# A fused convolution and two feed-forward layers on one core: weight decoding moved wholly into the convolution, its inverse stages one chunk later, the filter's second transform in three reduced-precision passes

## The chip, the cores and the metric

One core of a Trainium2 chip runs the whole program in one launch. The metric is device time in microseconds (us), start to end of one execution. The median of three runs of the kernel before is 3027.79 us (3024.66 to 3028.4).

## The reference

The reference has three parts, one after the other. `L = 2 * S`, with S = 12480 positions, 2 batches and 128 channels.

```
h_filt = (maximum(pos_emb @ w1, 0) @ w2) * exp(-0.01 * pos)[:, None]
Uf = rfft(x * v, n=L, axis=1);  Hf = rfft(h_filt, n=L, axis=0)
y  = irfft(Uf * Hf, n=L, axis=1)[:, :S, :]
x1 = (x * y).reshape(24960, 128)
h  = x1 @ moe_w_in;   g = where(h > 0, h, exp(minimum(h, 0)) - 1);  x2 = g @ moe_w_out
h  = x2 @ moe2_w_in;  g = h * cos(h);                               out = g @ moe2_w_out
```

The feed-forward width is 2048. The four weight matrices arrive as 64-bit floats, as pairs of 32-bit words; the kernel has to turn them into 32-bit floats on the chip ("decoding").

## The kernel before, in words

The program has four stretches: the filter's taps (a small network, at the start), the convolution, layer 1 of the feed-forward part and layer 2.

**Convolution** (L310 to L434). The 128 channels are worked off in 32 chunks of four (`DC`, `NCH`). For each chunk there are three signals, written `k`: 0 and 1 are the two batches, 2 is the filter. Each goes through a two-step forward transform: `st_a` multiplies by a 98-row table on TensorE (tile `ps_a`), VectorE forms two products with the twiddle table (`za`, `zb`) and GpSimd (POOL) adds them (`z_t`); `st_b` multiplies by the 128-row table `dft_t` (tile `ps_b`). For `k` = 2 ScalarE (ACT) copies the result out as `hr` and `hi_f`; for `k` = 0 and 1 VectorE multiplies it with these in three instructions (`ya`, `ps_b`, `y_t`), ScalarE rounds `y_t` to the short format `yh`, and `lo_y` on POOL forms the rest `yl`. The inverse goes back in two steps: `st_c` multiplies `yh` and `yl` by the rounded tables `dft_h`, `dft_l` in three passes (tile `ps_c`), VectorE forms `wa` and `wb`, POOL adds them to `w_t`; `st_d` multiplies by `g_t` (tile `ps_d`), and VectorE multiplies by x (`at`, L407), which SP stores to `xt_d`. `prod` on POOL makes the inputs `u_t`. `st_a` and `st_b` use full 32-bit operands, `st_c` the short format (fp32r).

The order in each chunk's turn is a table written out by hand, `steps` (L424); each entry names a stage, how many chunks back it works, and `k`. The scheduler keeps program order on each engine. `ps_a`, `ps_b` and `ps_c` have one buffer each, `ps_d` two; `za`, `zb` and `w_t` have two, `wa` and `wb` one.

**Decoding** (class `Decode`, L96). A job takes 128 x n weights. VectorE works on the upper words (`sg`, `mag`, `keep`, `bits`, `av`, `pw`; L119 to L141), ScalarE squares and converts (`sq`, `lf`), and the value is split into a rounded part `hi` and a rest `lo`, which go to `w_d` in DRAM (some also whole, to `wf_d`). Layer 1's 16 jobs of 256 columns run in the convolution, one step at a time (`next(now, None)`, L432) after nine of the entries of a turn, VectorE's six instructions and POOL's three or four each. Layer 2's eight jobs of 512 columns run inside layer 1 of the feed-forward part (`arena`, L592; `next(later, None)`, L626), with two more subtractions and additions on VectorE (L161, L163).

**Feed-forward layers** (L496 to L639). Tiles of 480 tokens (`T`), 52 per layer; each has eight blocks `m` of two 128-wide slices. `gemm1` makes `h_ps` in three passes, ScalarE and VectorE make the activation, POOL splits it into `gh` and `gl` (L93, L94), `gemm2` accumulates `o_ps` five blocks later (`LAG`). `split_x` on POOL makes `xh`, `xl` of the next tile in the middle of a tile. The first weights of layer 1 are loaded by ScalarE's queue (L611), with the first two `x_in`; the first of these waits for the stores of `xt_d`.

```
steps = ((st_a, 0, 2), (st_b, 1, 1), (lo_y, 1, 0), (st_d, 2, 1), (prod, 0, 1), (st_a, 0, 0),
         (lo_y, 1, 1), (prod, -1, 0), (st_c, 1, 0), (st_b, 0, 2), (st_a, 0, 1),
         (st_c, 1, 1), (st_b, 0, 0), (st_d, 1, 0))
```

Of the kernel before, what the change touches and what calls it, by code (L numbers as in the profile page):

```python
# [74 lines left out]
def hyena_moe_kernel(ctx: ExitStack, tc: tile.TileContext, x, v, pe, w1, w2,  # L75
# [20 lines left out]
    class Decode:  # L96


        def __init__(self, alloc, n, layer, which, q):
# [25 lines left out]
        def split(self):  # L125
            self.hi, self.lo = self.t("hi", F32R), self.t("lo", F32R)
            if not self.wide:
                self.av = self.raw
                copy_r(self.hi, self.raw)
                yield  # L130
                return
            keep, bits, self.av, pw, self.bv = (self.t("keep", I32), self.t("bits", I32), self.t("av", F32),
                                                self.t("pw", I32), self.t("bv", F32))
            nc.vector.tensor_scalar(keep, self.sq, TINY * TINY, -1.0, op0=ALU.is_ge, op1=ALU.mult)
            yield
            nc.vector.scalar_tensor_tensor(bits, self.mag, 0x40000000, self.sg,
                                           op0=ALU.bitwise_xor, op1=ALU.bitwise_or)
# [8 lines left out]

        def store(self):
            l, wh, n, p = self.layer, self.which, self.n, self.o
            nc.sync.dma_start(w_d[l, wh, 0, :, p:p + n], self.hi.bitcast(F32))
            for m in FULL[l] if wh else ():  # L150
                o = m * 256 - p
                if 0 <= o < n:
                    full = self.av[:, o:o + 256]
                    if self.wide:
                        full = self.t("full", F32)[:, 0:256]
                        nc.gpsimd.tensor_tensor(full, self.av[:, o:o + 256], self.bv[:, o:o + 256], op=ALU.add)
                        yield
                    nc.sync.dma_start(wf_d[l, m], full)
            if self.wide:
                dv = self.t("dv", F32)  # L160
                self.e.tensor_tensor(dv, self.av, self.hi.bitcast(F32), op=ALU.subtract)  # L161
                yield
                self.e.tensor_tensor(self.lo, dv, self.bv, op=ALU.add)  # L163
            else:
                nc.gpsimd.tensor_tensor(self.lo, self.av, self.hi.bitcast(F32), op=ALU.subtract)
            yield
            nc.sync.dma_start(w_d[l, wh, 1, :, p:p + n], self.lo.bitcast(F32))

        def run(self):
            for part in (self.words, self.split, self.store):  # L170
                yield from part()

    with tc.manual_schedule():
        with ExitStack() as cs:
# [132 lines left out]
            with ExitStack() as vs:  # L307
# [370 lines left out]
```

## Time and profile before

| | |
|---|---|
| median of three runs | 3027.79 us |
| profiled execution: device time | 3032.04 us |
| profiled execution: span, first to last instruction | 3030.2 us |
| mean granted TensorE clock | 0.993 of full |
| busy share of the span: TensorE, its weight loads, VectorE, ScalarE, POOL | 98%, 76%, 85%, 66%, 85% |
| convolution, first `st_a` to the last store landed | 50.68 to 745.18 us |
| layer 1, first `h_ps` | 740.19 us |

The busy shares are means over four stretches with different limits, so the profile has to be read stretch by stretch. TensorE's busy time counts matmuls whose ends are modelled; a share near 100% over a stretch means that it never ran dry there.

### The profile page before, as it was taken

The page shows a single profiled execution, that of the slowest core. Times are in us where ns is not written, and L with a number is a line of the kernel's source. Part 1 is how long each engine was busy: PE and PEld are TensorE (multiplying, and loading weights), DVE is VectorE, ACT ScalarE, POOL GpSimd, SP SyncE. Part 2 cuts the span into 40 slices and gives each one's busy share as a digit, 9 for nine tenths or more (in the row PEclk, how much of TensorE's full clock was granted, in tenths as well). Part 3 has the DMA queues.
Part 4 walks back from the last instruction along what each step waited for, and adds up shares of the span by engine and source line. Part 5 has one row for each costly group of instructions (what it writes and reads, how often), then busy time and mean ns, then how long its engine had stood idle before and what let it go on. Part 6 is the DMA issues. An engine that isn't in the chain of part 4 may idle for free.

```text
span 3030.2 us, 38341 instructions
## 1 busy us (share of the span) xinstructions
PE 2966.4 (98%) x13140; PEld 2317.9 (76%) x13140; DVE 2587.9 (85%) x3272; ACT 2006.6 (66%) x3076; POOL 2575.1 (85%) x1632
## 2 busy tenths in 40 slices
PE   8999999998999999999999999999999999999999
PEld 6777677775777777888888887787888878888887
DVE  5999987876999998888888888788888888888887
ACT  2111111112887888888888888788888888888887
POOL 4888877775898998888888888888888888888888
PEclk9999999998999999999999999999999999999999
DMA  3232322222011100000000001000000000000000
GB/s 103 76 84 78 87 63 64 63 53 88 24 38 38 45 21 10 14 10 14 10 14 11 14 11 40 23 14 10 14 11 13 11 14 10 14 11 14 11 14 14
DMA packets 79635, 96.16 MB, mean 32 GB/s; under 512 B 5722, under 2 KB 63096, under 8 KB 79442
## 3 DMA queue, kind: packets, MB, share of 16 engines
q1 hardware_dynamic: 74016, 88.07, 10.0%
q10 hardware_dynamic: 5426, 5.65, 0.6%
q8 instruction: 105, 1.72, 0.2%
q14 instruction: 88, 0.72, 0.1%
HBM read 59.16 MB, written 34.54 MB: 31 GB/s over the span
## 4 chain that ended last, share of the span: by engine, by line
PE 83%; DVE 12%; issue 2%; ACT 2%; POOL 1%; DMA 0%; POOLq 0%; ACTq 0%; DVEq 0%
PE o_ps L573 34%; PE h_ps L504 32%; PE ps_b L356 6%; PE ps_c L387 4%; PE ps_d L405 2%; PE ps_a L336 2%; DVE e L519 2%; DVE e L521 2%; DVE wb L391 1%; DVE wa L391 1%; DVE ya L368 1%; DVE av L139 1%; ACT e L515 1%; DVE ps_b L369 1%; DVE zb L341 1%
## 5 line engine op out<-in xcount | busy, mean ns | idle before, releaser
L94 POOL TENSOR_TENSOR gl<-e,gh 128x960 fp32r<-128x960 f32 x624 | 1414.7, 2274 | 127.3 <-ACT gh L85 92.6
L504 PE MATMUL h_ps<-xh,w 128*128 128x480 f32 x3328 | 1074.8, 404 | 26.6 <-DVE e L521 22.6
L504 PEld LDWEIGHTS h_ps<-xh,w 128*128 128x128 f32 x3328 | 623.4, 188 | 220.6 <-issue 73.0
L573 PE MATMUL o_ps<-gh,w 128*128 128x480 f32 x2496 | 746.7, 380 | 0.0
L534 DVE SCALAR_TENSOR_TENSOR e<-e,h_ps 128x960 f32<-128x960 int32 x416 | 480.2, 1154 | 201.6 <-ACT e L532 146.9
L504 PE MATMUL h_ps<-xl,w 128*128 128x480 f32 x1664 | 632.8, 380 | 0.1
L519 DVE SCALAR_TENSOR_TENSOR e<-e,t_ps 128x480 f32<-128x480 f32 x832 | 534.4, 651 | 96.2 <-ACT t_ps L517 87.6
L515 ACT ACTIVATE e<-h_ps 128x480 f32<-128x480 f32 x832 | 473.0, 569 | 173.4 <-PE h_ps L504 143.7
L532 ACT ACTIVATE e<-h_ps 128x960 int32<-128x960 f32 x416 | 404.2, 972 | 200.0 <-PE h_ps L504 197.0
L573 PEld LDWEIGHTS o_ps<-gh,w 128*128 128x128 f32 x2496 | 468.9, 188 | 76.1 <-issue 0.8
L93 POOL TENSOR_SCALAR gh<-e 128x960 fp32r<-128x960 f32 x416 | 422.9, 1017 | 114.8 <-DVE e L521 88.9
L517 ACT ACTIVATE t_ps<-h_ps 128x480 f32<-128x480 f32 x832 | 476.4, 573 | 15.6 <-DVE e L519 15.5
L573 PE MATMUL o_ps<-gl,w 128*128 128x480 f32 x1248 | 476.4, 382 | 3.0 <-POOL gl L94 2.9
L541 ACT ACTIVATE e<-e,half_pi 128x960 f32<-128x960 f32 x416 | 453.6, 1090 | 0.3 <-DVE e L534 0.3
L521 DVE SCALAR_TENSOR_TENSOR e<-e,h_ps 128x480 f32<-128x480 f32 x624 | 377.6, 646 | 0.0
L573 PE MATMUL o_ps<-gf,wf 128*128 128x480 f32 x832 | 368.6, 565 | 0.0
L543 DVE TENSOR_TENSOR e<-e,h_ps 128x960 f32<-128x960 f32 x312 | 358.1, 1148 | 1.3 <-ACT e L541 1.2
L504 PEld LDWEIGHTS h_ps<-xl,w 128*128 128x128 f32 x1664 | 313.0, 188 | 53.3 <-POOL xl L94 0.8
L85 ACT ACTIVATE yh<-y_t 128x720 fp32r<-128x720 f32 x64 | 51.5, 805 | 411.2 <-DVE y_t L371 335.9
L573 PEld LDWEIGHTS o_ps<-gl,w 128*128 128x128 f32 x1248 | 234.7, 188 | 42.3 <-POOL gl L94 5.0
L356 PE MATMUL ps_b<-z_t,dft_t 128*128 128x360 f32 x768 | 254.3, 475 | 8.8 <-DVE y_t L371 8.2
L344 POOL TENSOR_TENSOR z_t<-za,zb 128x720 f32<-128x720 f32 x96 | 141.9, 1478 | 114.2 <-DVE zb L341 114.2
(94 smaller groups left out, 3479.0 us busy)
## 6 DMA issues: line engine op xcount, KB each, us to landing
x_t<-in_x SPq DMA_DIRECT2D x32, 392.0 KB
v_t<-in_v SPq DMA_DIRECT2D x32, 392.0 KB
xt_d<-at SPq DMA_DIRECT2D x64, 196.0 KB
out<-ot SPq DMA_DIRECT2D x52, 240.0 KB
x_in<-xt_d SPq DMA_DIRECT2D x50, 240.0 KB
w_d<-x SPq DMA_DIRECT2D x16, 256.0 KB
w<-w_d ACTq DMA_DIRECT2D x14, 256.0 KB
w<-w_d SPq DMA_DIRECT2D x14, 256.0 KB
```

The lines of the kernel that those rows point to most:

```text
L93: ENG[plan[0]].tensor_scalar(hi, full, 1.0, 0.0, op0=ALU.mult, op1=ALU.add)
L94: ENG[plan[1]].tensor_tensor(lo, full, hi.bitcast(F32), op=ALU.subtract)
L356: nc.tensor.matmul(ps[:, r, 0:n], dft_t[:, sl], z[:, q], start=j == 0, stop=j == 1)
L504: nc.tensor.matmul(h[:, 0:T], a, b, start=k == 0, stop=k == 2)
L515: nc.scalar.activation(u[:, e], hs[e][:, 0:T], AF.Exp)
L517: nc.scalar.activation(ts[e][:, 0:T], hs[e][:, 0:T], AF.Tanh, scale=0.5)
L519: nc.vector.scalar_tensor_tensor(u[:, e], u[:, e], 1.0, ts[e][:, 0:T], op0=ALU.add, op1=ALU.mult)
L521: nc.vector.scalar_tensor_tensor(gt[:, e], u[:, e], 0.0, hs[e][:, 0:T], op0=ALU.min, op1=ALU.max)
L532: nc.scalar.activation(kq, hv, AF.Copy, scale=1.0 / TWO_PI, bias=0.25)
L534: nc.vector.scalar_tensor_tensor(rr, kq, -TWO_PI, hv, op0=ALU.mult, op1=ALU.add)
L541: nc.scalar.activation(rr, rr, AF.Sin, bias=half_pi)
L573: nc.tensor.matmul(o, a, b[:, e], start=f == 0 and k == 0, stop=f == NFT - 1 and k == len(mm) - 1)
```

## The change

- `Decode` has a first half `bits` with four VectorE instructions instead of six (the flush of tiny values is now made by ScalarE's Sign, with the constant `below`), and a second half `parts` with three POOL instructions and one rounding copy.
- All 32 jobs, of both layers and 256 columns wide, run in the convolution; `arena` and its calls are gone. One `bits` step stands between the two VectorE products of each `st_a` and of `st_c` with `k` = 1: four per turn. Three `low` entries per turn issue the POOL half.
- `st_b` of the filter (`k` = 2) is done in three passes: ScalarE rounds `z_t` to `zh`, `lo_z` on POOL forms `zl`, and 12 fp32r matmuls replace four 32-bit ones.
- `st_c` with `k` = 1 and both `st_d` work a chunk further back, and the order of the turn is another. The loads of the chunk after next are issued at the end of a turn, not in its middle.

```diff
-            nc.scalar.activation(self.sq, top.bitcast(F32), AF.Square)
-            nc.vector.tensor_scalar(self.sg, top, -2147483648, None, op0=ALU.bitwise_and)
...
+            nc.scalar.activation(sq, top.bitcast(F32), AF.Square)
+            nc.vector.tensor_scalar(self.mag, top, 0x0FFFFFFF, 3, op0=ALU.bitwise_and, op1=ALU.logical_shift_left)
+            yield
+
+            keep = sq.bitcast(I32)
+            nc.scalar.activation(keep, sq, AF.Sign, scale=-1.0, bias=below)
+            nc.vector.scalar_tensor_tensor(self.mag, top, -2147483648, self.mag,
+                                           op0=ALU.bitwise_and, op1=ALU.bitwise_or)
             yield
             nc.scalar.activation(self.lf, low.bitcast(U32), AF.Copy, scale=2.0 ** -52)
-            nc.vector.tensor_scalar(self.mag, top, 3, 0x7FFFFFFF, op0=ALU.logical_shift_left, op1=ALU.bitwise_and)
+            nc.vector.scalar_tensor_tensor(self.mag, self.mag, 0x40000000, keep,
+                                           op0=ALU.bitwise_xor, op1=ALU.bitwise_and)
             yield
+            nc.vector.scalar_tensor_tensor(self.pw, self.mag, -8388608, self.mag,
+                                           op0=ALU.bitwise_and, op1=ALU.bitwise_and)
+            yield
+
+        def parts(self):
+
+            if self.wide:
+                self.full = self.t("full", F32)
+                nc.gpsimd.tensor_tensor(self.lf, self.lf, self.pw.bitcast(F32), op=ALU.mult)
+                yield
+                nc.gpsimd.tensor_tensor(self.full, self.mag.bitcast(F32), self.lf, op=ALU.add)
+            hi, lo = self.t("hi", F32R), self.t("lo", F32R)
+            copy_r(hi, self.full)
             yield
+            nc.gpsimd.tensor_tensor(lo, self.full, hi.bitcast(F32), op=ALU.subtract)
+            nc.sync.dma_start(w_d[l, wh, 0, :, p:p + n], hi.bitcast(F32))
...
             yield
+            nc.sync.dma_start(w_d[l, wh, 1, :, p:p + n], lo.bitcast(F32))
...
                     for q, t in ((0, t1), (1, t2)):
                         nc.vector.tensor_tensor(bank2(t), ps[:, :, 0:n],
                                                 tw_t[:, q:q + 1].to_broadcast([NB, 2, n]), op=ALU.mult)
+                        if q == 0:
+                            next(bits, None)
...
+                    if k == 2:
+                        zh = p1.tile([NB, 2, DC * NF], F32R, name="zh")
+                        copy_r(zh, z)
+                        z = (z, zh)
...
-                            nc.tensor.matmul(ps[:, r, 0:n], dft_t[:, sl], z[:, q], start=j == 0, stop=j == 1)
+                            if k == 2:
+                                zh, zl = z
+                                mm = ((dft_h, zh), (dft_l, zh), (dft_h, zl))
+                            else:
+                                mm = ((dft_t, z),)
...
+                        if q == 0 and k == 1:
+                            next(bits, None)
...
-                        if f in (st_a, st_c, st_d, lo_y) and p > 0:
-                            next(now, None)
-                        if f is prod and back < 0:
-                            load(p + 2)
+                    load(p + 2)
+                for _ in bits:
+                    pass
+                for _ in rest:
+                    pass
...
-                if 8 <= n < 200:
-                    next(later, None)
```

The new table of a turn:

```
steps = ((prod, 0, 1), (low, 0, 0), (lo_y, 1, 0), (st_a, 0, 2), (low, 0, 1), (st_c, 2, 1), (lo_z, 0, 2),
         (st_b, 1, 1), (lo_y, 1, 1), (st_a, 0, 0), (st_d, 2, 0), (low, 0, 2), (st_c, 1, 0), (st_b, 0, 2),
         (prod, -1, 0), (st_a, 0, 1), (st_d, 2, 1), (st_b, 0, 0))
```

VectorE, in the middle of a turn of the convolution, before: `st_a` of batch 1, two decode instructions behind it, `st_c` of batch 1, a third behind that, and `st_a` of the next chunk's filter.

```order
L341 TENSOR_TENSOR za<-ps_a,tw_t 128x720
L341 TENSOR_TENSOR zb<-ps_a,tw_t 128x720
L136 SCALAR_TENSOR_TENSOR bits<-mag,sg 128x256
L139 TENSOR_TENSOR av<-bits,keep 128x256
L391 TENSOR_TENSOR wa<-ps_c,ti_t 90x1024
L391 TENSOR_TENSOR wb<-ps_c,ti_t 90x1024
L141 TENSOR_SCALAR pw<-av 128x256
L341 TENSOR_TENSOR za<-ps_a,tw_t 128x720
L341 TENSOR_TENSOR zb<-ps_a,tw_t 128x720
```

The same engine in the changed kernel, from the last products of `st_c` (batch 0) over `st_a` of batch 1 and the products of `st_b` to the next turn's `st_a` of the filter.

```order
L399 TENSOR_TENSOR wb<-ps_c,ti_t 90x1024
L330 TENSOR_TENSOR za<-ps_a,tw_t 128x720
L128 SCALAR_TENSOR_TENSOR mag<-raw,mag 128x256
L330 TENSOR_TENSOR zb<-ps_a,tw_t 128x720
L417 TENSOR_TENSOR at<-ps_d,x_t 98x512
L376 TENSOR_TENSOR ya<-ps_b,hr 128x720
L377 TENSOR_TENSOR ps_b<-ps_b,hi_f 128x2x360
L379 TENSOR_TENSOR y_t<-ya,ps_b 128x720
L330 TENSOR_TENSOR za<-ps_a,tw_t 128x720
L132 SCALAR_TENSOR_TENSOR mag<-mag,sq 128x256
L330 TENSOR_TENSOR zb<-ps_a,tw_t 128x720
```

And on through `st_c` of batch 1, the products of `st_b`, and `st_a` of batch 0.

```order
L399 TENSOR_TENSOR wa<-ps_c,ti_t 90x1024
L135 SCALAR_TENSOR_TENSOR pw<-mag 128x256
L399 TENSOR_TENSOR wb<-ps_c,ti_t 90x1024
L376 TENSOR_TENSOR ya<-ps_b,hr 128x720
L377 TENSOR_TENSOR ps_b<-ps_b,hi_f 128x2x360
L379 TENSOR_TENSOR y_t<-ya,ps_b 128x720
L330 TENSOR_TENSOR za<-ps_a,tw_t 128x720
L123 TENSOR_SCALAR mag<-raw 128x256
L330 TENSOR_TENSOR zb<-ps_a,tw_t 128x720
```

The decode instructions, which stood one or two together behind a pair of products, now stand one at a time inside each pair: behind `za` and ahead of `zb`, or behind `wa` and ahead of `wb`.

POOL, one turn before (from `lo_y` of batch 1; `bv`, `dv` and `lo` are the decode):

```order
L328 TENSOR_TENSOR yl<-y_t,yh 128x720
L317 TENSOR_TENSOR u_t<-x_t,v_t 98x512
L398 TENSOR_TENSOR w_t<-wa,wb 90x1024
L344 TENSOR_TENSOR z_t<-za,zb 128x720
L144 TENSOR_TENSOR bv<-lf,pw 128x256
L398 TENSOR_TENSOR w_t<-wa,wb 90x1024
L161 TENSOR_TENSOR dv<-av,hi 128x256
L163 TENSOR_TENSOR lo<-dv,bv 128x256
```

POOL, the same length in the changed kernel, from `st_a` of batch 1 on (`full`, `lo` and `lf` are the decode):

```order
L335 TENSOR_TENSOR z_t<-za,zb 128x720
L306 TENSOR_TENSOR u_t<-x_t,v_t 98x512
L145 TENSOR_TENSOR full<-mag,lf 128x256
L317 TENSOR_TENSOR yl<-y_t,yh 128x720
L335 TENSOR_TENSOR z_t<-za,zb 128x720
L150 TENSOR_TENSOR lo<-full,hi 128x256
L408 TENSOR_TENSOR w_t<-wa,wb 90x1024
L346 TENSOR_TENSOR zl<-z_t,zh 128x720
L317 TENSOR_TENSOR yl<-y_t,yh 128x720
L335 TENSOR_TENSOR z_t<-za,zb 128x720
L143 TENSOR_TENSOR lf<-lf,pw 128x256
L408 TENSOR_TENSOR w_t<-wa,wb 90x1024
```

POOL has one more 720-column instruction (`zl`) per turn, the three decode instructions are spread out, and a `w_t` now comes right ahead of `zl` and, once per turn, at the end ahead of `u_t`.

## Rows read from the trace of the kernel before

**Rows 1.** Windows, turns with and without decoding: length, busy PE, PEld, DVE, ACT, POOL.

```profile
103.03:124.27 21.24, 20.44 (x105) 15.15 (x105) 19.68 (x25) 3.86 (x8) 17.57 (x13) 1.00 0.29 82
438.64:458.89 20.25, 20.25 (x106) 15.20 (x105) 16.15 (x19) 2.80 (x6) 14.98 (x10) 1.00 0.23 59
```

**Rows 2.** Chain of waits, convolution's start and end: start us, us, what.

```profile
50.68 2.12 PE ps_a L336 x8
...
90.20 2.66 PE ps_b L356 x8
...
716.78 4.35 PE ps_b L356 x8
...
730.05 1.22 DVE wa L391
```

**Rows 3.** Timeline of VectorE, a turn with decoding: start us, us, instruction.

```profile
177.79 0.91 DVE L368 TENSOR_TENSOR ya<-ps_b,hr 128x720 f32<-128x720 f32 x1 [0.41 <-PE ps_b L356]
...
180.38 0.29 DVE L122 TENSOR_SCALAR mag<-raw 128x256 int32<-128x256 int32 x1
...
181.89 0.90 DVE L341 TENSOR_TENSOR za<-ps_a,tw_t 128x720 f32<-128x720 f32 x1
182.70 0.89 DVE L341 TENSOR_TENSOR zb<-ps_a,tw_t 128x720 f32<-128x720 f32 x1
183.52 0.41 DVE L136 SCALAR_TENSOR_TENSOR bits<-mag,sg 128x256 int32<-128x256 int32 x1
184.03 1.50 DVE L139 TENSOR_TENSOR av<-bits,keep 128x256 int32<-128x256 int32 x1
185.46 1.21 DVE L391 TENSOR_TENSOR wa<-ps_c,ti_t 90x1024 f32<-90x1024 f32 x1
186.59 1.21 DVE L391 TENSOR_TENSOR wb<-ps_c,ti_t 90x1024 f32<-90x1024 f32 x1
```

**Rows 4.** Timeline of POOL around that turn: start us, us, instruction.

```profile
171.02 0.72 POOL L144 TENSOR_TENSOR bv<-lf,pw 128x256 f32<-128x256 f32 x1
172.29 2.42 POOL L398 TENSOR_TENSOR w_t<-wa,wb 90x1024 f32<-90x1024 f32 x1 [0.56 <-DVE wb L391]
...
178.74 1.71 POOL L328 TENSOR_TENSOR yl<-y_t,yh 128x720 fp32r<-128x720 f32 x1
...
183.74 1.51 POOL L344 TENSOR_TENSOR z_t<-za,zb 128x720 f32<-128x720 f32 x1 [1.93 <-DVE zb L341]
185.21 1.91 POOL L328 TENSOR_TENSOR yl<-y_t,yh 128x720 fp32r<-128x720 f32 x1
```

**Rows 5.** Chain of waits, a turn without decoding, then layer 1.

```profile
438.64 2.85 PE ps_c L387 x24
441.49 2.42 PE ps_b L356 x8
...
1331.23 1.31 PE h_ps L504 x6
```

**Rows 6.** Costliest groups, convolution: weight loads of `st_c`, busy us, mean ns.

```profile
L387 PEld LDWEIGHTS ps_c<-dft_h,yh 128*90 128x90 f32 x253 | 39.6, 157 | 10.2 <-ACT hi_f L362 10.2
```

**Rows 7.** Timeline of POOL in layer 1: `xh` of tiles 2, 16 and 21.

```profile
779.21 0.59 POOL L93 TENSOR_SCALAR xh<-x_in 128x480 fp32r<-128x480 f32 x1
...
1107.08 0.60 POOL L93 TENSOR_SCALAR xh<-x_in 128x480 fp32r<-128x480 f32 x1
...
1214.83 0.59 POOL L93 TENSOR_SCALAR xh<-x_in 128x480 fp32r<-128x480 f32 x1
```

**Rows 8.** Windows, layer 1 while layer 2's weights are decoded.

```profile
779.21:1107.08 327.87, 310.89 (x1290) 238.38 (x1289) 321.42 (x514) 267.32 (x515) 294.49 (x179) 1.00 0.12 36
```

**Rows 9.** Costliest groups of the whole run: rounding copy of `y_t`.

```profile
L85 ACT ACTIVATE yh<-y_t 128x720 fp32r<-128x720 f32 x64 | 51.5, 805 | 411.2 <-DVE y_t L371 335.9
```

**Rows 10.** Chain of waits where convolution hands over to layer 1.

```profile
738.83 6.35 DMA xt_d<-at
...
746.73 0.57 ACT e L515
```

More of the change, by code (lines that the diff above doesn't have):

```diff
@@ L110, in __init__, with bits @@
                                   w[o:o + n, :].rearrange("(k p) d -> p k d", p=128))
-        def words(self):
+        def bits(self):
             if not self.wide:
+                self.full = self.raw
+                yield
                 return
@@ L152, in store @@
                 if 0 <= o < n:
[L153 to L165, printed above, removed]
+                    nc.sync.dma_start(wf_d[l, m], self.full[:, o:o + 256])
             yield
[L167 to L171, printed above, removed]
+            nc.sync.dma_start(w_d[l, wh, 1, :, p:p + n], lo.bitcast(F32))
+    one = ctx.enter_context(tc.tile_pool(name="one", bufs=1))
+    below = one.tile([128, 1], F32, name="below")
     with tc.manual_schedule():
+        nc.vector.memset(below, BELOW)
         with ExitStack() as cs:
@@ L355, in st_b @@
                         for j, (sl, q) in enumerate(prs[r]):
[L356 removed]
+                            if k == 2:
[3 more added lines that the diff above has]
+                                mm = ((dft_t, z),)
+                            for i, (a, b) in enumerate(mm):
+                                nc.tensor.matmul(ps[:, r, 0:n], a[:, sl], b[:, q], start=j == 0 and i == 0,
+                                                 stop=j == 1 and i == len(mm) - 1)
                     if k == 2:
@@ L410, in alloc, with bits_of_all @@
                 def alloc(name, dt):
-                    return (p2 if name == "raw" else p1).tile([128, 256], dt, name=name, tag=f"d_{name}")
-                def first_layer():
-                    jobs = [(0, w, q) for w in range(2) for q in range(DFF // 256)]
+                    return (p1 if name == "sq" else p2).tile([128, 256], dt, name=name, tag=f"d_{name}")
+                jobs = [(l, w, q) for l in range(2) for w in range(2) for q in range(DFF // 256)]
+                ready = []
+                def bits_of_all():
                     nxt = Decode(alloc, 256, *jobs[0])
@@ L419, in first_layer, with parts_of_all, low @@
                             nxt = Decode(alloc, 256, *jobs[i + 1])
-                        yield from dec.run()
-                now = first_layer()
+                        yield from dec.bits()
+                        ready.append(dec)
+                def parts_of_all():
+                    for i in range(len(jobs)):
+                        while len(ready) <= i:
+                            yield
+                        yield from ready[i].parts()
+                bits, rest = bits_of_all(), parts_of_all()
+                def low(c, k):
+                    next(rest, None)
                 prod(0, 0)
-                steps = ((st_a, 0, 2), (st_b, 1, 1), (lo_y, 1, 0), (st_d, 2, 1), (prod, 0, 1), (st_a, 0, 0),
-                         (lo_y, 1, 1), (prod, -1, 0), (st_c, 1, 0), (st_b, 0, 2), (st_a, 0, 1),
-                         (st_c, 1, 1), (st_b, 0, 0), (st_d, 1, 0))
+                steps = ((prod, 0, 1), (low, 0, 0), (lo_y, 1, 0), (st_a, 0, 2), (low, 0, 1), (st_c, 2, 1), (lo_z, 0, 2),
+                         (st_b, 1, 1), (lo_y, 1, 1), (st_a, 0, 0), (st_d, 2, 0), (low, 0, 2), (st_c, 1, 0), (st_b, 0, 2),
+                         (prod, -1, 0), (st_a, 0, 1), (st_d, 2, 1), (st_b, 0, 0))
                 for p in range(NCH + 2):
                     for f, back, k in steps:
-                        if 0 <= p - back < NCH:
+                        if 0 <= p - back < NCH or f is low:
                             f(p - back, k)
-                        if f in (st_a, st_c, st_d, lo_y) and p > 0:
-                            next(now, None)
-                        if f is prod and back < 0:
-                            load(p + 2)
+                    load(p + 2)
[3 more added lines that the diff above has]
+                    pass
         wp = ctx.enter_context(tc.tile_pool(name="wp", bufs=1))
@@ L587, in reload @@
                 layers[1].load(nc.sync, wh, m)
-        ARENA = T * 20
-        ASIZE = (B * S - ARENA) // 2
-        def arena():
-            jobs = [(1, w, q) for w in range(2) for q in range(DFF // 512)]
-            for i, job in enumerate(jobs):
-                free = [ARENA + i % 2 * ASIZE]
-                def alloc(name, dt):
-                    n = 512 * (2 if name == "raw" and dt != F32 else 1)
-                    t = x1[:, free[0]:free[0] + n]
-                    free[0] += n
-                    return t if dt == F32 else t.bitcast(dt)
-                dec = Decode(alloc, 512, *job)
-                for _ in range(4):
-                    yield
-                yield from dec.run()
-        later = arena()
         for wh in range(2):
```

32 lines of the change are left out of this document (8 added, 24 removed).

## Prediction

> **What bounds the kernel now.** I read the busy time by stage first, then the chain of waits inside each stage, then the timelines of VectorE and POOL, because the page's shares are means over four stretches. In the convolution a turn takes 21.24 us while layer 1's weights are decoded and 20.25 us after that [rows 1]. In the second kind TensorE is busy all the time and VectorE 16.15 us: TensorE is the bound. In the first kind VectorE is busy 19.68 us and TensorE runs dry for 0.8 us: VectorE and its decode steps are the bound. From the first `st_b` of turn 2 to that of turn 32 there are 626.6 us [rows 2], 20.9 per turn on average.
>
> In layer 1 a tile takes (1214.83 - 1107.08) / 5 = 21.55 us once the decoding of layer 2 is over, and the 14 tiles before that take 327.87 us [rows 7]. In that stretch VectorE is busy 321.42 us and TensorE only 310.89 [rows 8]. So the arena costs 327.87 - 14 x 21.55 = 26.2 us.
>
> A decode step costs VectorE more than its work. `bits`, with POOL idle, takes 0.41 us. `av`, of the same size, issued at 184.03, takes 1.50: POOL's `z_t` began at 183.74 and ended at 185.25, and `av` ended 0.28 later [rows 3, 4]. The next `yl` on POOL began with `z_t`'s end and took 1.91 instead of 1.71 [rows 4]. I read this so: a VectorE instruction that takes everything from SBUF waits until the POOL instruction in progress has ended, and then goes ahead of the next. Products that read PSUM keep 0.9 whatever POOL does.
>
> **Part 1: the arena goes.** Eight jobs leave layer 1. TensorE then sets the pace there, as in the tiles behind them: -26.2 us. Nothing else waits on these jobs.
>
> **Part 2: a turn of the convolution.** Three engines are near each other, so I sum each.
>
> TensorE: the filter's `st_b` took 2.42 us [rows 5]. Three passes are 12 matmuls of 360 columns; six of 480 take 1.31 us in layer 1 [rows 5], 0.218 each, so 0.164 for 360 and 1.97 for the twelve. The turn's sum becomes 20.25 - 2.42 + 1.97 = 19.8 us.
>
> POOL: 14.98 busy [rows 1], plus `zl` like `yl` 1.71, plus three decode instructions of 0.72 [rows 4]: 18.9, and some 0.2 more for each decode step that gets in ahead of it, 19.6 at most.
>
> VectorE: 16.15 plus four steps. What each costs follows from what POOL does when it is issued. From the starts in [rows 3], a `za` or `zb` holds the queue 0.81 us, a `wa` or `wb` 1.13, the three products of `st_b` together 180.38 - 177.79 = 2.59.
> - In `st_a` of the filter: POOL has finished `u_t` and one decode instruction and waits for `yl`, which needs `y_t`, 0.90 us, and ScalarE's copy, 0.81 [rows 9]. The step comes before. Cost 0.4.
> - In `st_c` of batch 1: `z_t` starts about 1.05 after the start of `zb` or, if `yl` is still running, later. The step is issued 0.81 + 1.13 = 1.94 after it, in the middle of `z_t`. Cost between 0.8 and 1.8; I take 1.5, as for `av`.
> - In `st_a` of batch 0: POOL runs `w_t`, 2.42, from about 1.29 after the start of `wb`, then `zl`, 1.71, to 5.4. The step is issued at 1.13 + 2.59 + 0.81 = 4.5. Cost 1.0.
> - In `st_a` of batch 1: `wb` of `st_c` is the instruction before `za`, so `w_t` has just begun: it ends at 3.7, the step is issued at 1.94. Cost 2.0 with its own tail.
>
> Sum 4.9, so VectorE has 16.1 + 4.9 = 21.0 us per turn. That is above the other two, so I take **21.0** as the turn. It takes the place of 20.9: 30 full turns x 0.1 = +3 us. The ends of this term: if no step ever waits, four times 0.4 gives 17.8 on VectorE and TensorE's 19.8 decides; if the first step too waits behind a `yl`, 22.6.
>
> ScalarE adds a copy of 0.81 and three more small ones to a load of 2.80 [rows 1]: hidden under a turn of 21. Without that cover, `zh` and `zl` stand between `z_t` and the filter's `st_b`. The order I laid out by hand has `st_b` waiting about 0.9 us for `zl`, which VectorE's 21.0 covers. SP's queue: all 32 turns now have the raw loads and two decode stores that the first 17 had; the loads of x and v, moved behind the last product, are needed some 19 us later. Nothing there is late.
>
> **Part 3: the ends.** Before, turns 0 and 1 take 90.20 - 50.68 = 39.5 us to the `st_b` of turn 2, and from the `st_b` of turn 32 to the end of the last `st_c` 730.05 - 716.78 = 13.3 [rows 2]. With the inverse a chunk later, turn 1 lacks a `st_c` and a `st_d`; VectorE's part there is about 15.5 instead of 20.8, while turn 0 grows by 1 for `zh` and `zl`: -4. The last turn gains what the second lost, of which about 2 are not covered: +2.
>
> Behind the last `st_c` the old kernel needs 16.7 us to ScalarE's first Exp, 6.35 of them for the last store of `xt_d` [rows 2, 10]. In the new order the last job's rounding copy stands on ScalarE's queue ahead of all weight loads of layer 1, and the first `x_in` stands behind eight of them. Rows of before don't show this; below it is 0, since the store's landing covers it, above 8 (all eight loads after the landing). Since the last POOL half is three instructions of 0.72 and a copy, some 3 us behind `w_t`, I take +3.
>
> **Sum:** -26.2 + 3 - 4 + 2 + 3 = -22 us. Against the profiled execution, 3032.0, that is 3010; it lies 4.2 above the median of the runs shown, so the forecast for the median is **3005 us**.
>
> **Rivals.**
> - *POOL is idle when the steps come* (20%). If POOL catches up so that it waits for `zb` and `wb`, the steps cost 0.4 and TensorE bounds: a turn of 20.0, 30 x (20.0 - 21.0) = -30, 2975 us. For: it has 2 us to spare per turn. Against: two of the four steps come right after the instruction that starts a `z_t` or `w_t`.
> - *The first step misses its gap* (10%, slower). It is issued 0.81 + 0.82 = 1.63 after the start of `y_t`, and `yl` can begin at 0.90 + 0.81 and two hand-overs of 0.1, 1.9. If it is 0.3 us later, `yl` goes first and the step waits 1.6 more: 22.6 a turn, 30 x 1.6 = +48, 3053 us. The change turns slower from a turn of 21.7 on, so it suffices that this happens in half of the turns.
> - *The weight loads of the three passes aren't hidden* (4%, slower). With each load of 0.157 or more [rows 6] ahead of its matmul, the twelve take 12 x (0.164 + 0.157) = 3.85, TensorE's turn is 21.7 and with the wait for `zl` 22.6: 3050. Against it: 24 matmuls of `st_c`, each with such a load, take 2.85 us [rows 5], 0.119 each for 256 columns.
> - *The hand-over is worse or the three-engine coupling costs more, and it comes out even* (9%): 3025.
>
> A rule of the Trainium skill speaks for the third of these: the page "TensorE: Matmul & The Clock Gate" says in Part 3, "The mechanism", that a weight load overlaps matmuls in flight only when their row groups differ, and its section on LDWEIGHTS gives columns / 1.2 ns, 107 ns for 128 columns. By that the twelve would be about 12 x (150 + 107) = 3.1 us, an estimate from the page. The trace does not agree: a `st_c` matmul with its load takes 0.119 us, less than the load's own 0.157.
>
> **How the numbers follow.** The forecast case, a turn of 20.5 to 21.5, has 57% and spans 2988 to 3021 with the hand-over at its ends. The first rival lies below, to 2970. The range 2970 to 3030 holds these and the even case, and leaves out the two slower rivals. A measurement of this kernel can tell some 0.2%, 6 us, from no change. Faster by more than that: 57 + 20 and a little of the even case, 0.79. Within: 0.08. Slower: the two rivals less what they overlap, 0.13.
>
> **What would show it.** In the changed profile: `xh` steps of 21.55 from the first tiles of layer 1 on, with no VectorE bound; turns of 21.0, VectorE over 95% busy and TensorE near 94%; the step between `za` and `zb` of batch 1 at 2 us or more and that of the filter at 0.4; the twelve matmuls at about 2.0 us. Turns near 20 with steps of 0.4 show the first rival, steps of 2 us in the filter's `st_a` the second, a `ps_b` group of 3.8 us the third. The prediction is wrong in its base if layer 1's first 14 tiles stay above 21.6.

## The result, and the profile after

The changed kernel takes 3046.88 us (median of 4 runs, 3045.14 to 3048.95), the kernel before 3027.11 beside it. The ratio is 1.0067, with a 95% interval of 1.0049 to 1.0084: slower by 20 us (0.7%), where 22 less were forecast. The profiled execution took 3046.99 us (span 3045.2), against 3032.04 before.

The engines' line of the page, over the whole span:

```profile
PE 2948.4 (97%) x13268; PEld 2330.1 (77%) x13268; DVE 2660.9 (87%) x3241; ACT 2046.2 (67%) x3164; POOL 2650.1 (87%) x1700
```

Again the shares say little, so by stage. First layer 1, the POOL timeline, with `xh` of the tiles that [rows 7] shows (tiles 2 and 16):

```profile
820.72 0.60 POOL L95 TENSOR_SCALAR xh<-x_in 128x480 fp32r<-128x480 f32 x1
...
1122.34 0.59 POOL L95 TENSOR_SCALAR xh<-x_in 128x480 fp32r<-128x480 f32 x1
```

1122.34 - 820.72 = 301.62 us for the 14 tiles that took 327.87: 26.25 less, and 21.54 a tile. Then the convolution, by windows: one turn, and most of the stage (length, busy time of PE, PEld, DVE, ACT, POOL; granted clock, DMA share, GB/s).

```profile
302.83:325.13 22.30, 20.32 (x109) 15.53 (x108) 22.23 (x23) 4.96 (x10) 19.51 (x13) 1.00 0.29 84
100.00:725.00 625.00, 569.13 (x3030) 434.84 (x3029) 623.09 (x617) 139.16 (x281) 547.04 (x365) 1.00 0.28 79
```

VectorE is busy 623 of 625 us. It bounds the whole stage, in turns of 22.3 us where [rows 1] had 21.24 and 20.25. The four decode steps in VectorE's costliest groups, 300 to 500 us (busy, mean ns of one, idle before):

```profile
L123 DVE TENSOR_SCALAR mag<-raw 128x256 int32<-128x256 int32 x9 | 24.7, 2745 | 0.0
...
L128 DVE SCALAR_TENSOR_TENSOR mag<-raw,mag 128x256 int32<-128x256 int32 x9 | 18.9, 2096 | 0.0
...
L135 DVE SCALAR_TENSOR_TENSOR pw<-mag 128x256 int32<-128x256 int32 x9 | 14.4, 1599 | 0.0
...
L132 DVE SCALAR_TENSOR_TENSOR mag<-mag,sq 128x256 int32<-128x256 int32 x9 | 3.7, 416 | 0.0
```

They stand in `st_a` of batch 0 (L123), `st_a` of batch 1 (L128), `st_c` of batch 1 (L135) and the filter's `st_a` (L132). L123 is the one out of line: 2.7 us. Its surroundings, timelines of VectorE, POOL and ScalarE:

```profile
517.62 0.91 DVE L379 TENSOR_TENSOR y_t<-ya,ps_b 128x720 f32<-128x720 f32 x1
518.44 0.90 DVE L330 TENSOR_TENSOR za<-ps_a,tw_t 128x720 f32<-128x720 f32 x1
519.26 2.76 DVE L123 TENSOR_SCALAR mag<-raw 128x256 int32<-128x256 int32 x1
521.95 0.90 DVE L330 TENSOR_TENSOR zb<-ps_a,tw_t 128x720 f32<-128x720 f32 x1
```

```profile
516.03 2.42 POOL L408 TENSOR_TENSOR w_t<-wa,wb 90x1024 f32<-90x1024 f32 x1 [0.62 <-DVE wb L399]
518.42 1.75 POOL L346 TENSOR_TENSOR zl<-z_t,zh 128x720 fp32r<-128x720 f32 x1
520.13 1.74 POOL L317 TENSOR_TENSOR yl<-y_t,yh 128x720 fp32r<-128x720 f32 x1
522.99 1.47 POOL L335 TENSOR_TENSOR z_t<-za,zb 128x720 f32<-128x720 f32 x1 [1.11 <-DVE zb L330]
```

```profile
518.62 0.81 ACT L87 ACTIVATE yh<-y_t 128x720 fp32r<-128x720 f32 x1 [3.25 <-DVE y_t L379]
```

The step is issued at 519.26, 0.91 before `zl` ends, and ends at 522.02, 0.15 after `yl`. At `zl`'s end POOL went on with `yl` and VectorE did not get in; so in 30 of the 31 turns with a `zl`; in the other one, near the start, the step was issued 0.58 before `zl`'s end and got in. The step holds VectorE from 519.26 to 521.95, 2.69 us of the turn.

### The profile page after: what moved, and what is told of

Read it like the earlier page. It is cut to its first block, busy times and chain, and to the rows that moved or that the text cites. A ratio compares the mean times of both kernels' runs of the same rounds, so it can differ in the third digit from the quotient of the medians.

```text
span 3045.2 us, 38862 instructions
## 1 busy us (share of the span) xinstructions
PE 2948.4 (97%) x13268; PEld 2330.1 (77%) x13268; DVE 2660.9 (87%) x3241; ACT 2046.2 (67%) x3164; POOL 2650.1 (87%) x1700
## 4 chain that ended last, share of the span: by engine, by line
PE 75%; DVE 13%; POOL 6%; issue 4%; ACT 1%; DMA 0%; POOLq 0%; DVEq 0%; SPq 0%; ACTq 0%
PE o_ps L597 38%; PE h_ps L528 36%; POOL w_t L408 2%; DVE wa L399 2%; POOL u_t L306 2%; DVE wb L399 2%; DVE za L330 2%; POOL z_t L335 1%; DVE pw L135 1%; DVE zb L330 1%; DVE ps_b L377 1%; DVE ya L376 1%; DVE at L417 1%; PE h_ps L263 1%; DVE mag L123 0%
## 5 line engine op out<-in xcount | busy, mean ns | idle before, releaser
L528 PE MATMUL h_ps<-xh,w 128*128 128x480 f32 x3328 | 1074.1, 404 | 16.8 <-POOL xh L95 11.2
L543 DVE SCALAR_TENSOR_TENSOR e<-e,t_ps 128x480 f32<-128x480 f32 x832 | 543.1, 654 | 125.1 <-ACT t_ps L541 114.8
L95 POOL TENSOR_SCALAR gh<-e 128x960 fp32r<-128x960 f32 x416 | 414.9, 997 | 112.7 <-DVE e L545 103.1
L597 PEld LDWEIGHTS o_ps<-gf,wf 128*128 128x128 f32 x832 | 157.0, 189 | 100.8 <-issue 88.6
L87 ACT ACTIVATE gh<-e 128x960 fp32r<-128x960 f32 x208 | 208.0, 1000 | 11.3 <-PE o_ps L597 11.3
```

What stands on the lines that cost most here:

```text
L95: ENG[plan[0]].tensor_scalar(hi, full, 1.0, 0.0, op0=ALU.mult, op1=ALU.add)
L528: nc.tensor.matmul(h[:, 0:T], a, b, start=k == 0, stop=k == 2)
L543: nc.vector.scalar_tensor_tensor(u[:, e], u[:, e], 1.0, ts[e][:, 0:T], op0=ALU.add, op1=ALU.mult)
L597: nc.tensor.matmul(o, a, b[:, e], start=f == 0 and k == 0, stop=f == NFT - 1 and k == len(mm) - 1)
```

## The experiments

The theory: VectorE's steps wait for POOL, and L123 waits through two instructions because the three passes put `zl` there. The rivals: the step's form; the twelve matmuls; the later inverse stages. A turn is taken from one `wa` to the same one of the next turn, mean of 23 turns in the middle of the convolution. Each time is of one run, but those of the change and of e10_psum_all are medians of four. The kernel before, run beside them, took 3026.1 us with e1, e2, e3 and e5, 3026.49 with e4, e6, e7 and e8, 3026.49 (median of 9, from 3023.56 to 3031.8) with e9, e10 and the second time of e2, and 3023.94 with e11.

| run | us | turn, us | mean duration of the steps from 300 to 500 us, in us: `st_a` 0, `st_a` 1, `st_c` 1, filter's `st_a` |
|---|---|---|---|
| the change | 3046.88 | 22.30 | 2.75, 2.10, 1.60, 0.42 |
| e1_form | 3052.73 | 22.44 | 2.88, 2.09, 1.60, 0.42 |
| e2_one_pass | 2976.28 | 20.07 | 0.28, 2.04, 1.60, 0.42 |
| e3_no_steps | 2961.63 | 19.57 | none |
| e4_three_in_c1 | 3012.79 | 21.26 | moved, 3.3 in all |
| e5_three_in_c0 | 3046.66 | 22.33 | moved, 6.3 in all |
| e6_two_in_c1 | 3060.42 | 22.94 | moved, 6.0 in all |
| e7_zl_idle | 3042.43 | 22.24 | 2.72, 2.06, 1.60, 0.42 |
| e8_no_zl | 2968.69 | 19.85 | 0.28, 2.10, 1.60, 0.42 |
| e9_psum_two | 2982.29 | 20.08 | 0.42, 0.41, 1.60, 0.42 |
| e10_psum_all | 2962.24 | 19.57 | 0.42, 0.42, 0.41, 0.42 |
| e11_zl_after_yl | 3115.41 | 24.61 | 0.28, 0.48, 1.60, 0.42 |

**The form of the step, or its place (e1_form).**

```diff
-            nc.vector.tensor_scalar(self.mag, top, 0x0FFFFFFF, 3, op0=ALU.bitwise_and, op1=ALU.logical_shift_left)
+            nc.vector.scalar_tensor_tensor(self.mag, top, 3, held["ones"], op0=ALU.logical_shift_left, op1=ALU.bitwise_and)
...
+                held["ones"] = p1.tile([128, 256], I32, name="ones")
+                nc.vector.memset(held["ones"], 0x7FFFFFF8)
```

> The decode step in batch 0's st_a (L123 of the changed kernel, a TENSOR_SCALAR that reads the raw words) is written as a SCALAR_TENSOR_TENSOR like the other three, with the same result: (top << 3) & a tile that holds 0x7FFFFFF8. In the changed kernel this step took 2.74 us, 30 of 31 times to the end of the yl behind the zl that runs when it is issued, while I had counted 1.0, to the end of zl. Theory A, the form decides which engine goes first where a POOL instruction ends: the step now gets in between zl and yl, takes about 1.0, the turn falls from 22.30 to 22.3 - 1.7 = 20.6 us and the time by 31 x 1.7 = 50 us to about 2995. Theory B, the place decides (POOL has its next instruction ready when zl ends): the step stays at 2.7, the turn at 22.3, the time at 3047.

The group of the step, 300 to 500 us:

```profile
L125 DVE SCALAR_TENSOR_TENSOR mag<-raw,ones 128x256 int32<-128x256 int32 x9 | 25.9, 2879 | 0.0
```

2.88 us, 30 times through `zl` and `yl`. It isn't the form of the instruction; the expectation's theory B, the place, holds.

**Without the three passes (e2_one_pass).** `zh`, `zl` and the entry `lo_z` go; `mm = ((dft_t, z),)` for all `k`.

> The filter's second transform goes back to four 32-bit matmuls, so zh and zl are gone; all else is the changed kernel. TensorE's sum per turn rises from 19.8 to 20.25 us, POOL's falls by 1.7. If VectorE's turn is long because the step in batch 0's st_a waits through zl and yl (2.7 us), it now waits for the end of w_t or of yl alone: 0.4 to 1.9, a turn of 20.3 to 21.5 and 2985 to 3022 us. If instead that step waits for two POOL instructions whatever they are, or the later inverse stages make the turn long, the turn stays above 22 and the time above 3035.

The step's group, the POOL timeline around it (the step is issued at 515.86) and the window 300 to 500:

```profile
L123 DVE TENSOR_SCALAR mag<-raw 128x256 int32<-128x256 int32 x10 | 2.8, 284 | 0.0
```

```profile
512.63 2.43 POOL L400 TENSOR_TENSOR w_t<-wa,wb 90x1024 f32<-90x1024 f32 x1 [0.63 <-DVE wb L391]
516.10 1.72 POOL L317 TENSOR_TENSOR yl<-y_t,yh 128x720 fp32r<-128x720 f32 x1 [1.04 <-ACT yh L87]
```

```profile
300.00:500.00 200.00, 198.99 (x1038) 151.30 (x1037) 197.49 (x220) 41.40 (x90) 175.39 (x121) 1.00 0.31 88
```

POOL has ended `w_t` and waits for `yh` when the step comes: 0.28 us in all 32 turns. The time, 2976, is lower than I expected at the least, since I had not counted an idle POOL there. Run again, five times (e2_again):

> The run without the three passes once more, timed in five rounds: TensorE's 20.07 us per turn bound it, so 2976 within 3 us, 0.983 of the kernel before. If its first time was chance, it lies nearer to 3000.

2976.68 us, ratio 0.9836 (0.9822 to 0.9849). So all of the change but the three passes is worth 50 us.

**Which part of the three passes (e7_zl_idle, e8_no_zl).** In the first `zl` is made and left unread; in the second the twelve matmuls stay and `zl` is not made (`lo_z` also leaves the table of steps).

```diff
-                    zz[c, k] = (zh, zl)
+                    zz[c, k] = z
...
-                            if k == 2:
-                                zh, zl = z
-                                mm = ((dft_h, zh), (dft_l, zh), (dft_h, zl))
...
+                            mm = ((dft_t, z),)
```

```diff
-                                zh, zl = z
-                                mm = ((dft_h, zh), (dft_l, zh), (dft_h, zl))
+                                zh = z[1]
+                                mm = ((dft_h, zh), (dft_l, zh), (dft_l, zh))
```

> Of the three passes only the preparation stays: ScalarE makes zh and POOL makes zl, which nobody reads, and the filter's second transform is four 32-bit matmuls on z_t. Theory A, POOL's zl is the cause: zl runs when the step of batch 0's st_a is issued and yl follows it without a gap, so the step still takes 2.7 us, VectorE's turn stays at 22.3 us (TensorE's 20.25 is under it) and the time at 3047. Theory B, the twelve matmuls and st_b's wait for zl are the cause: as without the three passes, a turn of 20.1 us and 2976.

> The twelve matmuls stay, but zl is not made: the third pass takes zh once more with the small table dft_l, so the filter's values are off in the last places. Theory A (POOL's zl is the cause): the step of batch 0's st_a finds POOL waiting for yh and takes 0.3 us; VectorE's turn is 16.1 + 3.9 = 20.0 us at most, TensorE's 19.8, so 19.7 to 20.0 us, 31 x 2.3 to 2.6 us below the changed kernel: 2966 to 2976. Theory B (the matmuls): a turn of 22.3 us, 3047.

The step's groups, of e7_zl_idle and of e8_no_zl:

```profile
L123 DVE TENSOR_SCALAR mag<-raw 128x256 int32<-128x256 int32 x9 | 24.5, 2717 | 0.0
```

```profile
L123 DVE TENSOR_SCALAR mag<-raw 128x256 int32<-128x256 int32 x10 | 2.8, 285 | 0.0
```

With `zl` and without its matmuls the step takes 2.7 us, with the matmuls and without `zl` 0.28. So POOL's `zl` alone makes the wait, and the two runs show it from both sides.

**Without the steps (e3_no_steps).** The four VectorE instructions are left out, `mag` and `pw` are fixed tiles.

> VectorE's four decode instructions per turn are left out (two fixed tiles stand in for their results, so the feed-forward layers work with wrong weights); ScalarE's and POOL's part of the decoding stays. If the steps' waits are all that makes the turn 22.3 us, VectorE has some 15.7 us of its own and the turn falls to TensorE's 19.8 or POOL's, 19.5 to 20.2: 31 x 2.2 = 68 us less, about 2978. If the later inverse stages or the longer chain of zh and zl bound the turn too, it stays above 21 us and the time above 3005.

```profile
300.00:500.00 200.00, 200.00 (x1108) 160.15 (x1107) 164.84 (x186) 51.19 (x103) 190.79 (x134) 1.00 0.32 92
```

The window shows TensorE busy all the time and VectorE 165 of 200 us. The turn of 19.57 is TensorE's own, a little under the 19.8 of the prediction. The 2978 expected stood for a turn 2.2 us shorter than 22.3, so 20.1; the turn is 0.5 shorter than that, and the time, 2961.63, 16 lower. The later inverse stages, and `st_b` behind `zh` and `zl`, bound nothing above that. (By the two tables of steps, of the two `st_d` only batch 0's moved a chunk further back; batch 1's stood two back before.)

**Other places for the steps (e5_three_in_c0, e6_two_in_c1, e4_three_in_c1).** The number of steps in each place is set by hand, in `A_STEPS` for `st_a` and `C_STEPS` for `st_c`, by `k`: (0, 0, 1) and (3, 0) in e5, (0, 1, 1) and (0, 2) in e6, (0, 0, 1) and (0, 3) in e4.

```diff
                         if q == 0:
-                            next(bits, None)
+                            for _ in range(A_STEPS[k]):
+                                next(bits, None)
...
-                        if q == 0 and k == 1:
-                            next(bits, None)
+                        if q == 0:
+                            for _ in range(C_STEPS[k]):
+                                next(bits, None)
```

> The four steps are moved: one stays in the filter's st_a, three stand in a row between the two products of batch 0's st_c, none in the st_a of the batches or in batch 1's st_c. One wait for the POOL instruction in progress is then shared by three steps of 0.4 us. Theory (VectorE's waits for POOL bound the turn): the steps cost 0.4 + at most 1.9 + 3 x 0.4 = 3.5 us instead of 6.5, more likely 2, and the turn falls to 20.0 to 20.5, TensorE's or POOL's bound: 2978 to 2992 us. Rival (each step is passed by a POOL instruction of its own, so three in a row wait three times): 0.4 + 3 x 1.8 = 5.8, a turn of 21.6, 3025 us.

> The changed kernel with one of its four steps moved: none in batch 0's st_a, two in a row in batch 1's st_c, all else as it was, zl too. Theory (one step in the wrong place): VectorE's turn loses the step's 2.66 us and gains 0.33 beside the one that waits there already, 22.3 - 2.3 = 20.0 us; TensorE's 19.8 is just below: 31 x 2.3 = 71 us less, 2976. Rival (VectorE, once faster there, comes to another step at a worse moment, as with three steps in batch 0's st_c, where the filter's step then took 3.08 us in place of 0.42): 21.5 us or more, above 3020.

> One step stays in the filter's st_a, three stand in a row in batch 1's st_c, none in the st_a of the batches. If the three share one wait for z_t: 1.53 + 2 x 0.33 + 0.33 = 2.5 us for the four, VectorE 18.3, and TensorE bounds at 19.7 to 19.8 us: 31 x 2.5 = 78 us less, 2967. Rival (without the step in batch 1's st_a, which covered w_t, the filter's step comes while POOL still works off u_t and the decode instruction ahead of yl, and is passed by all of them): 3.1 us there, 1.5 + 0.7 + 3.1 = 5.3, a turn of 21.1 us or more, above 3008.

Step groups of e5_three_in_c0 (L130 now stands in the filter's `st_a`, L134 first in batch 0's `st_c`), then of e6_two_in_c1 (L137 in batch 1's `st_a`):

```profile
L130 DVE SCALAR_TENSOR_TENSOR mag<-raw,mag 128x256 int32<-128x256 int32 x9 | 27.7, 3083 | 0.0
...
L134 DVE SCALAR_TENSOR_TENSOR mag<-mag,sq 128x256 int32<-128x256 int32 x9 | 22.1, 2458 | 0.0
```

```profile
L137 DVE SCALAR_TENSOR_TENSOR pw<-mag 128x256 int32<-128x256 int32 x9 | 32.5, 3606 | 0.0
```

The theories' sums failed in both; of the rivals, that of e5 failed too, and that of e6 held. Steps in a row do share one wait: behind L134's 2.46 the other two of e5 took 0.43 and 0.29. But a step that no longer waits brings VectorE earlier to the next one, and that then met POOL instructions that stood back to back: in e5 the filter's step, with 3.08 us in place of 0.42, in e6 the step of batch 1's `st_a`, 3.61 in place of 2.10, through `w_t` and the `u_t` behind it in 28 of 31 turns. In e6 two steps in a row also show a wait of 1.0 us for ScalarE's Sign between them. In e4 the steps cost 3.3 us and VectorE is no longer the bound (busy 179.5 of 200 us); the waits of TensorE there, 300 to 500 us (total, times, longest):

```profile
PE ps_b L366 <- POOL zl L349: 7.5, 10, 0.8
```

Three steps ahead of `wb` make `w_t`, and with it `zl` and the filter's `st_b`, late. So the expected 2967 was missed by 46 us. The rival's bounds (a turn of 21.1 us or more, above 3008) fit only by luck: the wait of 3.1 us that it named did not come.

**Operands outside SBUF (e9_psum_two, e10_psum_all).** The places stay, `zl` stays. `ps_d` gives one of its two buffers to a bank that holds `acc` and a constant.

```diff
-            nc.vector.tensor_scalar(self.mag, top, 0x0FFFFFFF, 3, op0=ALU.bitwise_and, op1=ALU.logical_shift_left)
+            nc.vector.tensor_scalar(held["acc"], top, 0x0FFFFFFF, 3, op0=ALU.bitwise_and, op1=ALU.logical_shift_left)
...
-            nc.vector.scalar_tensor_tensor(self.mag, top, -2147483648, self.mag,
+            nc.vector.scalar_tensor_tensor(held["acc"], top, -2147483648, held["acc"],
...
-            nc.vector.scalar_tensor_tensor(self.mag, self.mag, 0x40000000, keep,
+            nc.vector.scalar_tensor_tensor(self.mag, held["acc"], 0x40000000, keep,
...
-            nc.vector.scalar_tensor_tensor(self.pw, self.mag, -8388608, self.mag,
+            nc.vector.scalar_tensor_tensor(self.pw, self.mag, -8388608, held["all"].to_broadcast([128, 256]),
...
-                pd = vs.enter_context(tc.tile_pool(name="pd", bufs=2, space=PSUM))
+                pd = vs.enter_context(tc.tile_pool(name="pd", bufs=1, space=PSUM))
+                pk = vs.enter_context(tc.tile_pool(name="pk", bufs=1, space=PSUM))
...
+                bank = pk.tile([128, 512], I32, name="bank")
+                held["acc"], held["all"] = bank[:, 0:256], bank[:, 256:257]
+                nc.vector.memset(held["all"], -1)
```

This is e10; e9 moves only the first result, which the second step then reads.

> The changed kernel, three passes and all four places kept, but the step of batch 0's st_a writes its result to PSUM (ps_d gives up one of its two buffers for the bank), and the step of batch 1's st_a reads that from PSUM, so neither takes everything from SBUF any more. Theory (a step waits for POOL because its operands, all in SBUF, need what POOL's instruction holds): both cost about 0.35 us whatever POOL does, in place of 2.66 and 2.02; VectorE has 22.25 - 4.0 = 18.3 us, TensorE bounds at 19.7 to 19.9, 31 x 2.5 = 78 us less, 2964 to 2972. Rival 1 (it is the place in the order that makes VectorE wait, not the operands): 22.3 us a turn, 3047. Rival 2 (ps_d with one buffer holds TensorE up, or a step moved forward loses elsewhere, as with two steps in batch 1's st_c): 20.5 to 22.9 us.

> As the run before it, with the other two steps too: each of the four has one operand or its result in PSUM (the step in batch 1's st_c takes its second operand, a constant of ones, from there). Theory: the four cost 1.4 to 1.7 us together in place of 6.5, VectorE has 17.3 to 17.6 us per turn and TensorE bounds at 19.6 to 19.9: 2958 to 2970, at best 3 us below the run with two, since TensorE bounds both; faster than the kernel before by 2%. Rival (place, not operands): 22.3 us, 3047.

e9_psum_two, VectorE's groups:

```profile
L137 DVE SCALAR_TENSOR_TENSOR pw<-mag 128x256 int32<-128x256 int32 x10 | 16.0, 1599 | 0.0
...
L125 DVE TENSOR_SCALAR bank<-raw 128x256 int32<-128x256 int32 x10 | 4.2, 419 | 0.0
```

e10_psum_all, VectorE's groups, then the step and POOL's `zl` by their timelines, then the window:

```profile
L130 DVE SCALAR_TENSOR_TENSOR bank<-raw,bank 128x256 int32<-128x256 int32 x10 | 4.2, 420 | 0.0
L125 DVE TENSOR_SCALAR bank<-raw 128x256 int32<-128x256 int32 x10 | 4.2, 418 | 0.0
...
L137 DVE SCALAR_TENSOR_TENSOR pw<-mag,bank 128x256 int32<-128x256 int32 x10 | 4.1, 405 | 0.0
```

```profile
506.43 0.42 DVE L125 TENSOR_SCALAR bank<-raw 128x256 int32<-128x256 int32 x1
```

```profile
505.67 1.74 POOL L349 TENSOR_TENSOR zl<-z_t,zh 128x720 fp32r<-128x720 f32 x1
```

```profile
300.00:500.00 200.00, 200.00 (x1115) 160.75 (x1114) 176.00 (x226) 51.13 (x103) 190.99 (x134) 1.00 0.33 93
```

The step runs from 506.43 to 506.85, in the middle of `zl`, and waits for nothing: in the same place, beside the same POOL instruction, one operand or the result outside SBUF takes the wait away. Nor was it a wait for the result's tile to come free: L137, the step in `st_c` of batch 1, still writes `pw` in SBUF and falls from 1.60 to 0.41 us with its second input in PSUM. All four cost 1.7 us together, the turn is the 19.57 of the run without steps, and the time is **2962.24 us, ratio 0.9786 (0.9773 to 0.9799)**: faster than both kernels by 64 and 85 us. In e9 the step between `wa` and `wb` still waits, and `zl` comes later: TensorE waits 0.2 us a turn for it and the weight load ahead of the matmul 0.5, where e10 shows no such wait. The turn is 0.5 longer than in e10. So e9 missed its 2964 to 2972, and where I had expected at most 3 us between the two runs there were 20.

**The two neighbours on POOL exchanged (e11_zl_after_yl).** `(lo_z, 0, 2)` is moved behind `(lo_y, 1, 1)`.

> The changed kernel with two neighbours on POOL exchanged: yl of batch 1 first, zl of the filter behind it; the steps and the three passes stay as they were. In the changed kernel the step of batch 0's st_a was issued while zl ran, 0.9 us before its end, and waited through yl as well. Now POOL has ended w_t and waits for ScalarE's yh, 0.81 us behind y_t, when the step is issued 0.82 behind y_t's successor's start, so the step finds POOL idle. Theory (what POOL runs when a step is issued sets its price): 0.3 us in place of 2.7, VectorE 22.25 - 2.4 = 19.9 us. The filter's st_b then gets zl some 1.7 us later; where TensorE has no cover for that the turn is 19.7 + 1.7 = 21.4 us, so 20.0 to 21.4, 2976 to 3019. Rival (that step waits for a POOL instruction's end in any order): 1.7 us or more there, a turn of 21.3 with VectorE still the bound, 3016 or more.

The step costs 0.28 us in all 32 turns, as the theory has it, and not the rival's 1.7. But the time, 3115, is far above the theory's 2976 to 3019, and VectorE does not bound the turn (busy 147.7 us from 300 to 500). TensorE's timeline at the filter's `st_b`, and windows ahead of and in it:

```profile
518.40 0.67 PE L363 MATMUL ps_b<-zl,dft_h 128*128 128x360 f32 x1 [2.98 <-POOL zl L346]
518.87 0.50 PE L363 MATMUL ps_b<-zh,dft_h 128*128 128x360 f32 x1
519.17 0.50 PE L363 MATMUL ps_b<-zh,dft_l 128*128 128x360 f32 x1
```

```profile
511.70:515.00 3.30, 3.30 (x27) 3.03 (x26) 3.27 (x6) 0.92 (x2) 2.25 (x2) 1.00 0.00 0
515.00:518.40 3.40, 0.42 (x3) 0.12 (x2) 3.40 (x5) 0.22 (x1) 3.40 (x3) 0.90 0.30 83
518.40:521.00 2.60, 2.60 (x9) 2.60 (x10) 0.28 (x1) 0.00 (x0) 2.60 (x3) 0.50 0.07 23
```

TensorE waits 2.98 us for `zl`, and then its granted clock is 0.50, the lower of its two levels (1.2 of 2.4 GHz): the matmuls come 0.30 us apart, where the changed kernel had them 0.165 apart. The wait and the slow matmuls behind it are in place of the 1.7 us that I had counted.

## Why the prediction was wrong

- *Part 1, the arena.* -26.2 forecast, -26.25 measured. Right.
- *Part 2, TensorE and POOL.* TensorE's sum was 19.8; with VectorE out of the way it is 19.57. POOL was busy 19.51 us in the turn shown (18.9 to 19.6 forecast). The twelve matmuls took 1.98 us (1.97 forecast), by the chain of waits, so the third rival's 3.85 did not come:

```profile
75.40 1.98 PE ps_b L363 x12
```

- *Part 2, VectorE.* Three of the four steps came as counted: 0.33, 1.52 and 2.02 us from start to start against 0.4, 1.5 and 2.0. **The step that failed is "In `st_a` of batch 0 ... Cost 1.0".** It took 2.69. The prediction had the moment right (POOL in `zl`, 0.9 before its end) and the continuation wrong: it took over, as a rule, that a waiting VectorE instruction "goes ahead of the next". With 4.9 + 1.7 = 6.6 for the steps and 15.7 for the rest, VectorE has 22.3. The rest had been put at 16.1, VectorE's busy time in a turn with gaps [rows 1]; in the changed kernel's gapless turn it is 22.30 - 0.33 - 1.52 - 2.02 - 2.69 = 15.7 from start to start. That 0.4 hid a part of the error.
- *The reading behind it* was drawn from one `av` [rows 3, 4]. The trace of the kernel before held a counterexample that I did not look for. Timelines of VectorE and of POOL:

```profile
382.46 2.45 DVE L139 TENSOR_TENSOR av<-bits,keep 128x256 int32<-128x256 int32 x1
```

```profile
380.59 2.63 POOL L398 TENSOR_TENSOR w_t<-wa,wb 90x1024 f32<-90x1024 f32 x1
383.17 1.46 POOL L344 TENSOR_TENSOR z_t<-za,zb 128x720 f32<-128x720 f32 x1
```

  The same instruction, issued during `w_t`, took 2.45 us and ended 0.28 after the `z_t` behind it. Of the sixteen `av` of that trace fourteen got in after one POOL instruction, as the reading has it; this one and the next, each issued 0.76 before the end of a `w_t`, did not.
- *The second rival* had the right price and the wrong step. It gave 3053 us for a step that is passed by a `yl`, and the bound of 21.7 us from which the change turns slower; but it stood at the filter's `st_a`, where POOL was idle, and had 10%. The same question should have been put to each of the four steps.
- *Part 3.* From the first `ps_a` to the last `wa` the convolution takes 767.84 - 49.89 = 717.95 us against 730.05 - 50.68 = 679.37 [rows 2]: 38.6 more. Thirty turns of 1.4 make 42, so the ends give -3.4 (-2 forecast). The hand-over, from the last `wa` to the first Exp, is 788.93 - 767.84 = 21.1 us against 16.7 [rows 2, 10]: +4.4 (+3 forecast), through the last job's store and the first `x_in`. The rows are those of TensorE's timeline, of the chain of waits and of ScalarE's timeline:

```profile
49.89 1.31 PE L325 MATMUL ps_a<-fa_t,h_all 98*128 98x180 f32 x7 [1.83 <-DVE h_all L270]
```

```profile
767.84 1.22 DVE wa L399
...
776.74 5.97 DMA w_d<-hi
782.72 3.36 DMA x_in<-xt_d
```

```profile
788.93 0.57 ACT L539 ACTIVATE e<-h_ps 128x480 f32<-128x480 f32 x1 [14.60 <-DMA w<-w_d]
```

The sum as measured: -26.2 + 42 - 3.4 + 4.4 = +16.8; the convolution also began 0.8 earlier, so +16.0, against +15.0 between the two profiled executions. One term, 1.7 us in each of some thirty turns, turned a gain into a loss. The first rival (POOL idle at the steps, 2975) is what e2_one_pass shows at that one step; that its time comes so near is luck, since two of the other steps cost there what they cost in the changed kernel. Two small sums of the prediction are off and change nothing: the third rival's turn of 22.6 gives 3053, not 3050, and turns of 20.5 to 21.5 with the hand-over between 0 and 8 give 2987 to 3025, not 2988 to 3021.

The Trainium skill, page "SBUF — State Buffer", "Who interferes with whom", says that a VectorE instruction with two SBUF inputs, or in a mode that uses both of its ports, contends with POOL, and one with at most one SBUF input outside such a mode does not. The runs agree: beside `zl` the step took 0.42 us with its result in PSUM and 2.7 to 2.9 with all in SBUF. The 2.9 is the form with two inputs; that the form with one input, L123, is in such a mode was not shown by itself, though without a wait it is faster into SBUF (0.28) than into PSUM (0.42). The same section says that issue order decides who blocks. Here the measurement differs at an instruction's end: the step was issued at 519.26, `yh`, which `yl` needs, ended at 518.62 + 0.81 = 519.43, and still `yl` went first.

## What to carry to other kernels

A small VectorE instruction with all its operands in SBUF can cost as much as the POOL instructions that stand in a row when it is issued, so look at what follows on POOL as well as at what runs, and at every place of such an instruction. Moving the steps shifted VectorE to another collision in e5 and e6, and made `zl` late in e4; putting one operand or the result of each into PSUM took the wait away in all four places. Before adding an instruction to POOL, ask whose gap it fills: `zl` filled the one in which a decode step had been free.

## What the runs showed of the hardware

Which of the two gets in when a POOL instruction ends was not settled. In the changed kernel L128, issued 1.8 us before `w_t`'s end, got in ahead of `u_t` in all 30 turns in which `u_t` came next; in e6_two_in_c1 the step in that place (there it is L137, another of the four), issued 2.1 us before the end, was passed by `u_t` in 28 of 30. L135, issued 1.3 before the end of `z_t` (once 0.6), got in 30 times of 30 ahead of `lo`. L123 was passed 30 times with 0.9 left and got in once with 0.58. No threshold of the time left fits all of these. Nor does the next POOL instruction have to be ready first: `yl` went ahead though its input came 0.17 us after the step was issued. No rule was tried by itself.

A wait of 2.98 us of TensorE was followed by matmuls at half the clock (0.50); before it, in the same turn, the clock was 1.00. That made e11_zl_after_yl the slowest run of all, though its four steps took 2.8 us together, less than in any other run that has them but e10_psum_all.
